# Chunked attention and a gated convolution on one core: another way to decode float64 weights, and a new order of all steps

## The chip, the cores and the metric

The kernel runs on one core of a Trainium2 chip. The core has five engines that work through a queue of their own each: TensorE (PE; its weight loads are PEld), VectorE (DVE), ScalarE (ACT), GpSimd (POOL), and SyncE (SP), which here only issues DMAs. Engines wait for each other through semaphores. The metric is device time in microseconds (us) of one execution; the time before is the median of three runs.

## The reference

q, k and v have shape (4, 8, 768, 64): batch, heads, tokens, head size. Tokens are cut into 24 chunks of 32. Each chunk of queries sees a window of 64 keys: 8 memory keys, 16 to its left, its own 32, and 8 to its right.

```python
scores = scale * np.matmul(q_c, k_full.transpose(0, 1, 3, 2))
scores = scores - np.max(scores, axis=-1, keepdims=True)
a = np.exp(scores)
a = a / (np.sum(a, axis=-1, keepdims=True) + 1e-09)
out[:, :, c_start:c_end] = np.matmul(a, v_full)
...
for k in range(K):
    gate_pre += conv_w[k][None, None, :] * xp[:, k:k + S, :]
gate = 1.0 / (1.0 + np.exp(-gate_pre))
val = x @ w_val
return (gate * val @ w_out).astype(np.float32)
```

The attention output of all heads, x with 512 columns, goes through a causal convolution of five taps per column (the gate) and through two 512 x 512 matrices. These two, `w_val` and `w_out`, and the taps `conv_w` arrive as float64: the kernel reads each number as two 32-bit words and has to make a float32 of them on the chip.

## The kernel before, in words

**Attention by units.** A unit is one pair of heads over one span of tokens. Batch 0 is cut into two spans (256 and 512 tokens), the other batches have one of 768, which makes 20 units: 0 to 3 with 256 tokens, 4 to 7 with 512, 8 to 19 with 768. For a unit u the steps are: load k, q and v (`lk`, `lq`, `lv`), transpose k and q on TensorE (`tk`, `tq`) and copy them out of PSUM (`ek`, `eq`), scores (`sc`), maximum, shift and exponential (`mx`, `ss`, `ex`), transpose the weights of the softmax (`tp`, `ep`), times v (`va`), denominator, inverse, normalise (`nd`, `ni`, `nx`), transpose x (`tx`), split it into a high and a low float32r part (`xh`, `xl`), and five taps of the convolution on the vector engine (`cv`), then tanh (`ga`).

**Matrices by pieces.** Eight pieces of 256, 512 and 384 tokens go through the first matrix (`f1_n_...`), the gate (`h`), another split (`hh`, `hl`), the second matrix (`f2_n_...`), a copy out of PSUM (`oe`) and a store (`st`). Each product is three float32r matmuls: high times high, low times high, high times low.

**Weights.** A matrix is loaded in four row blocks of 128 x 512 float64, 512 KB each: `lw0` to `lw3` for `w_val`, `lw4` to `lw7` for `w_out`, with two raw buffers. Block `wv2`, say, is decoded in eight steps `wv21` to `wv28` (`float64_steps`, L344 to L402), then split into high and low (`wv2h`, `wv2`). Before the change, steps 1, 2, 3, 6 and 7 are vector passes over 128 x 512 (L355, L361, L366, L377, L382), steps 4 and 5 are on ScalarE (L371, L374), and step 8 is a float multiplication on GpSimd (L388).

**What sets the order.** The text `ORDER` lists every step once as `engine:step`; each engine issues its steps in the order in which they stand there, and DMAs are issued by the queue that is named (S for SP, G for POOL, A for ACT). `Plan.run` only sees to it that a step's needs stand ahead of it. An engine is strictly in order: if its next instruction waits, everything behind it waits too. PSUM has one buffer for transposes of q, k and the softmax (`t`), one for scores and value products (`a`), two for `tx` and three for the matrices.

Of the kernel before, what the change touches and what calls it, by code (L numbers as in the profile page):

```python
# [11 lines left out]
U32 = mybir.dt.uint32  # L12
AF = mybir.ActivationFunctionType
# [3 lines left out]
P = 128  # L17
# [3 lines left out]
NEG = -1.0e30  # L21
CAPS = dict(
# [52 lines left out]
V:wv0h V:nd0 G:wv0 V:wv13 T:tp1_0 S:lq3 V:ni0 A:mk2 A:ep1_0 V:nx0 S:lmv A:wv15 T:tk2_0 S:lk3 V:ek2_0
T:va1 T:tx0_0 V:nd1 V:ni1 A:xh0_0 V:wv21 T:tq2_0 A:eq2_0 A:mk3 S:lk4 G:wv18 S:lv2_0 V:nx1 S:lq5
V:wv22 A:wv1h V:mv4 V:cv0_0_4 T:tq3_0 A:eq3_0 G:mv3 V:wv23 T:sc2 V:mx2 A:wv24 V:wv26 T:tx1_0 V:ss2
V:cv0_0_0 A:cv1_0_4 G:lw3 G:wv1 S:lv2_1 T:tk3_0 A:ek3_0 V:cv0_0_1 A:ex2 T:tk4_0 A:wv25 S:lv3_0 T:sc3
V:wv27 V:xl0_0 S:lv3_1 A:ek4_0 T:tp2_0 V:cv1_0_0 A:ep2_0 V:mx3 V:cv1_0_1 V:ss3 V:wv31 A:wv34
V:cv0_0_2 V:cv1_0_2 G:wv28 T:va2 V:nd2 V:wv32 S:lw4 A:ex3 T:tq5_0 V:wv36 S:lq4 A:wv2h A:hs0 V:ni2  # L80
V:cv0_0 V:nx2 A:hs1 V:cv1_0 S:lk5 A:eq5_0 S:lk6 T:tp3_0 A:ep3_0 V:wv33 T:tx2_0 V:wv37 A:ga1 A:xh1_0
A:xh2_0 G:wv2 T:va3 T:tq4_0 S:lv4_1 T:f1_0_10 V:wo01 V:cv2_0_4 A:wv35 G:wv38 A:wo04 A:eq4_0 V:wo02
T:f1_0_00 V:nd3 V:wo03 V:ni3 T:tk5_0 V:xl1_0 A:wo05 A:ga0 S:lq6 G:mv5 A:ek5_0 V:nx3 S:lw5 A:wv3h
V:wo06 V:xl2_0 T:sc4 V:cv2_0_0 V:cv2_0_1 V:wo07 V:mx4 S:lv5_1 V:hs2 T:tx3_0 T:f1_0_11 V:ss4
A:cv3_0_4 S:lv4_0 T:tk6_0 T:sc5 A:ex4 V:cv3_0_0 A:ek6_0 T:tp4_0 T:f1_0_12 A:ep4_0 V:cv3_0_1 G:wv3
V:wo11 T:f1_0_01 V:mx5 V:wo12 V:ss5 A:wo14 A:xh3_0 V:cv2_0_2 T:tq6_0 V:wo13 A:eq6_0 V:cv2_0 A:ex5
# [12 lines left out]
V:wo36 T:tq9_0 T:f2_0_11 S:lq10 A:mk9 T:f1_1_01 A:eq9_0 V:wo37 G:wo2 A:cv6_1_4 A:wo35 V:nd7 V:xl6_0
T:tk9_0 T:f2_0_12 A:ek9_0 A:mk8 T:tk9_1 V:cv6_0_0 V:ni7 V:nx7 T:f2_0_02 G:wo38 V:cv6_1_0 A:xh6_1  # L100
A:ek9_1 V:cv6_0_1 V:cv6_1_1 A:wo3h V:xl6_1 G:wo3 T:tq9_1 A:eq9_1 T:sc8 V:cv6_1_2 V:cv6_0_2 V:cv6_1
V:cv6_0 T:tq10_0 T:f1_1_02 T:tx7_0 V:mx8 V:ss8 S:lv8_0 S:lk11 A:eq10_0 T:tx7_1 T:tq10_1 V:cv7_1_4
T:f2_0_03 A:xh7_0 A:eq10_1 V:xl7_0 G:mv10 V:hp7 T:sc9 A:ex8 A:oe0_0 T:tp8_0 V:xh7_1 A:cv7_0_4
V:cv7_1_0 S:lv8_1 V:xl7_1 S:lk10 A:ep8_0 T:f1_1_03 T:tp8_1 V:mx9 V:ss9 V:cv7_0_0 A:ep8_1 T:f2_0_13
# [79 lines left out]
def tile_chunked_attention_gated_conv(  # L184
# [794 lines left out]
```

## Time and profile before

| | |
|---|---|
| median of 3 runs | 269.98 us (266.08 to 270.07) |
| profiled execution, first to last instruction (span) | 269.1 us |
| PE busy | 238.3 us |
| DVE busy | 218.2 us |
| ACT busy | 127.9 us |
| POOL busy | 80.0 us |
| read from and written to HBM | 28.03 MB and 6.29 MB |

The page gives no other time for the profiled execution than its span, which is 0.9 us under the median of the runs. A busy share is a mean over the whole execution, and here the stretches differ: the table of stretches among the rows below is what to read first, each stretch with the busy time of each engine in it.

### The profile page before, as it was taken

What the parts mean: (1) busy time and instruction counts of PE and PEld (TensorE: products, weight loads), DVE (VectorE), ACT (ScalarE), POOL (GpSimd) and SP (SyncE); (2) the same over time, 40 slices, a digit from 0 to 9 for tenths busy, and PEclk for the clock granted to TensorE, in tenths of its full rate; (3) what the DMA queues carried; (4) which work ended last, traced back from release to release, by engine and by line L of the source; (5) the groups of instructions that cost most, each with busy time, mean ns of one, the idle gap of its engine ahead of it and who ended that gap; (6) DMA issues with size and microseconds to landing.
All of it is one profiled execution on the core that took longest, in us unless ns stands there. A gap on an engine that the chain in (4) does not pass through costs nothing.

```text
span 269.1 us, 9694 instructions
## 1 busy us (share of the span) xinstructions
PE 238.3 (89%) x4158; PEld 200.2 (74%) x4158; DVE 218.2 (81%) x462; ACT 127.9 (48%) x259; POOL 80.0 (30%) x93
## 2 busy tenths in 40 slices
PE   1576586796899996999999999999999999999994
PEld 1343376675678885778998878889998877899883
DVE  3799999899999995997976996999978989893310
ACT  4545574676866745555451515474432443521021
POOL 5473363146460044430105512200322120015100
PEclk9999997979999999999999999999999999999998
DMA  6788999499999899159897991398870061201213
GB/s 151 177 198 207 211 178 183 117 210 180 177 137 147 144 186 178 44 132 137 165 164 132 160 149 55 106 163 187 101 143 2 4 168 44 80 0 39 78 48 111
DMA packets 99601, 34.96 MB, mean 130 GB/s; under 512 B 96082, under 2 KB 96358, under 8 KB 99558
## 3 DMA queue, kind: packets, MB, share of 16 engines
q1 hardware_dynamic: 96710, 29.75, 62.7%
q0 software_dynamic: 1248, 4.20, 4.6%
q8 instruction: 33, 0.54, 0.9%
q10 hardware_dynamic: 1600, 0.39, 0.8%
q14 instruction: 10, 0.08, 0.1%
HBM read 28.03 MB, written 6.29 MB: 128 GB/s over the span
## 4 chain that ended last, share of the span: by engine, by line
PE 76%; DVE 12%; ACT 3%; issue 3%; DMA 3%; SPq 1%; POOL 1%; ACTq 0%; DVEq 0%
PE op L903 25%; PE vp L848 24%; PE sp L639 6%; PE xps L690 6%; PE tpx L750 4%; PE tq L569 4%; PE tk L569 4%; PE tp L569 4%; DVE gate L798 2%; DMA qn<-in_q_dram 2%; DVE e_wo L382 1%; DVE xn L713 1%; DVE e_wo L355 1%; SPq L493 1%; DMA craw<-in_moe_conv_w_dram 1%
## 5 line engine op out<-in xcount | busy, mean ns | idle before, releaser
L798 DVE SCALAR_TENSOR_TENSOR gate<-tpx,cw,gate 128x384 f32<-128x384 f32 (+9 forms) x144 | 79.3, 563 | 1.3 <-ACT gate L802 0.2
L264 POOL TENSOR_TENSOR hl<-h,hh 128x384 fp32r<-128x384 f32 (+2 forms) x25 | 26.0, 1044 | 107.6 <-DVE hh L249 55.2
L848 PE MATMUL vp<-xh,wv_hi 128*128 128x384 f32 (+2 forms) x128 | 49.1, 384 | 0.0
L848 PE MATMUL vp<-xl,wv_hi 128*128 128x384 f32 (+2 forms) x128 | 43.9, 343 | 0.0
L848 PE MATMUL vp<-xh,wv_lo 128*128 128x384 f32 (+2 forms) x128 | 43.9, 343 | 0.0
L903 PE MATMUL op<-wo_hi,hh 128*128 128x512 f32 (+1 forms) x100 | 41.9, 419 | 0.0
L903 PE MATMUL op<-wo_lo,hh 128*128 128x512 f32 (+1 forms) x100 | 38.6, 386 | 0.2 <-POOL wo_lo L264 0.2
L903 PE MATMUL op<-wo_hi,hl 128*128 128x512 f32 (+1 forms) x100 | 38.5, 385 | 0.0
L639 PE MATMUL sp<-kT,qT 64*32 64x64 f32 x1536 | 21.7, 239 | 8.7 <-DVE ss L664 3.9
L639 PEld LDWEIGHTS sp<-kT,qT 64*32 64x32 f32 x1536 | 17.6, 113 | 15.0 <-issue 8.4
L848 PEld LDWEIGHTS vp<-xh,wv_hi 128*128 128x128 f32 x128 | 25.0, 195 | 2.0
L854 DVE SCALAR_TENSOR_TENSOR h<-gate,vp 128x384 f32<-128x384 f32 (+2 forms) x32 | 17.2, 548 | 10.9 <-PE vp L848 9.4
L848 PEld LDWEIGHTS vp<-xh,wv_lo 128*128 128x128 f32 x128 | 25.1, 196 | 0.9
L848 PEld LDWEIGHTS vp<-xl,wv_hi 128*128 128x128 f32 x128 | 24.8, 194 | 0.9 <-DVE xl L264 0.2
L690 PE MATMUL xps<-v,pT 64*32 64x65 f32 x1536 | 21.1, 233 | 4.3 <-ACT pT L246 2.5
L690 PEld LDWEIGHTS xps<-v,pT 64*32 64x32 f32 x1536 | 17.3, 109 | 9.8 <-issue 6.1
L246 ACT COPY pT<-tp 128x384 f32<-128x384 f32 (+2 forms) x27 | 12.9, 479 | 23.5 <-PE tp L569 23.3
L569 PE MATMUL tk<-ident,kn 128*128 128x128 f32 x96 | 18.2, 304 | 6.2 <-ACT memT L246 2.6
L802 ACT ACTIVATE gate<-tpx,cw 128x384 f32<-128x384 f32 (+1 forms) x27 | 14.6, 549 | 15.1 <-PE tpx L750 10.0
L903 PEld LDWEIGHTS op<-wo_hi,hl 128*128 128x128 f32 x100 | 18.8, 188 | 4.0
L252 POOL COPY v<-mv 104x1536 f32<-104x1536 f32 (+2 forms) x12 | 17.4, 1458 | 11.5 <-issue 9.9
L569 PE MATMUL tq<-ident,qn 128*128 128x128 f32 x96 | 18.8, 311 | 2.1 <-DMA qn<-in_q_dram 0.9
(93 smaller groups left out, 423.7 us busy)
## 6 DMA issues: line engine op xcount, KB each, us to landing
qn<-in_q_dram SPq DMA_DIRECT2D x24, 192.0 KB
kn<-in_k_dram SPq DMA_DIRECT2D x24, 192.0 KB
v<-in_v_dram SPq DMA_DIRECT2D x24, 192.0 KB
v<-in_v_dram SPq DMA_DIRECT2D x23, 144.0 KB
out_dram<-o POOLq DMA_DIRECT2D x12, 256.0 KB, 4.0
out_dram<-o SPq DMA_DIRECT2D x11, 256.0 KB
raw_wo<-in_moe_w_out_dram SPq DMA_DIRECT2D x4, 512.0 KB
kn<-in_k_dram SPq DMA_DIRECT2D x12, 96.0 KB
```

Of the source, the lines that this page charges most:

```text
L246: return lambda: nc.scalar.copy(out(), in_())
L252: return lambda: nc.gpsimd.tensor_copy(out(), in_())
L264: return lambda: eng.tensor_tensor(out=out(), in0=a(), in1=b(), op=ALU.subtract)
L569: nc.tensor.transpose(U[name, i][:, (g - g0) * P : (g - g0 + 1) * P], src(g), ident)
L639: nc.tensor.matmul(U["sp"][CH * jc : CH * (jc + 1), j, g * WIN : (g + 1) * WIN], U["qT"][j * D : (j + 1) * D, g * P + CH * jc : g * P + CH ...
L690: nc.tensor.matmul(U["xps"][CH * jc : CH * (jc + 1), j, g * VW : (g + 1) * VW], U["pT"][j * D : (j + 1) * D, g * P + CH * jc : g * P + CH ...
L750: nc.tensor.transpose(U["x", i][:, o : o + P], U["xn"][:, g].rearrange("p j d -> p (j d)"), ident,)
L798: nc.vector.scalar_tensor_tensor(out=o, in0=i_, scalar=w, in1=o, op0=ALU.mult, op1=ALU.add)
L802: nc.scalar.activation(o, i_, AF.Copy, scale=w)
L848: nc.tensor.matmul(vp, w, x, start=ci == 0 and m == 0, stop=ci == NCT - 1 and m == 2)
L854: nc.vector.scalar_tensor_tensor(out=T["h", n, co][:, 0:nt], in0=bt[b, co]["gate"][:, t0 : t0 + nt], scalar=1.0, in1=T["vp", n, co][:, 0:n ...
L903: nc.tensor.matmul(op, x, w[:, ci, c0:c1], start=ci == 0 and m == 0, stop=ci == NCT - 1 and m == 2)
```

## The change

The decoding takes six passes in place of eight. ScalarE reads the high word as a float32, takes its absolute value times 2^-48 (`head`) and turns the low word into an integer of the last bits (`tail`). VectorE keeps the result in bounds (`bounds`), shifts it by three bits (`shifted`) and puts the sign in (`signed`). GpSimd adds the two as 32-bit integers (`rounded`). The small constants that the old passes needed, and their two steps, are gone.

```diff
-        def part1():
-            R["e"] = buf([np_, n], f"e{sfx}", f"e_{name}", U32)
...
-            nc.vector.tensor_scalar(
-                out=R["e"], in0=raw()[:, :, 1], scalar1=20, scalar2=0x7FF,
-                op0=ALU.logical_shift_right, op1=ALU.bitwise_and,
+        def head():
...
+            nc.scalar.activation(
+                R["e"], raw()[:, :, 1].bitcast(F32), AF.Abs, scale=2.0**-48
             )
-        def part2():
+        def bounds():
             nc.vector.tensor_scalar(
-                out=R["m"], in0=raw()[:, :, 1], scalar1=0xFFFFF, scalar2=None, op0=ALU.bitwise_and
+                out=R["e"], in0=R["e"], scalar1=FLOOR, scalar2=CEIL, op0=ALU.max, op1=ALU.min
             )
-        def part3():
-            nc.vector.scalar_tensor_tensor(
-                out=R["mf"], in0=raw()[:, :, 0], scalar=2.0**-32, in1=R["m"], op0=ALU.mult, op1=ALU.add
-        def part4():
-            nc.scalar.activation(R["ef"], R["e"], AF.Relu, bias=bias_e[0:np_], scale=E23)
-        def part5():
-            nc.scalar.activation(R["mf"], R["mf"], AF.Identity, bias=one[0:np_], scale=2.0**-20)
-        def part6():
+        def tail():
+            nc.scalar.activation(R["r"], raw()[:, :, 0], AF.Copy, scale=2.0**-29)
+        def shifted():
             nc.vector.tensor_scalar(
-                out=R["e"], in0=R["ef"], scalar1=255 * E23, scalar2=None, op0=ALU.min
+                out=e, in0=e, scalar1=3, scalar2=None, op0=ALU.logical_shift_left
             )
-        def part7():
+        def signed():
             nc.vector.scalar_tensor_tensor(
-                out=R["e"], in0=raw()[:, :, 1], scalar=0x80000000, in1=R["e"],
+                out=e, in0=raw()[:, :, 1], scalar=0x80000000, in1=e,
                 op0=ALU.bitwise_and, op1=ALU.bitwise_or,
             )
-        def part8(eng):
-            eng.tensor_tensor(out=R["mf"], in0=R["mf"], in1=R["ef"], op=ALU.mult)
+        def rounded():
+            nc.gpsimd.tensor_tensor(
+                out=R["r"], in0=R["e"].bitcast(I32), in1=R["r"], op=ALU.add
+            )
-        step(name + "1", {"V": part1}, after=[load[0], "bias"], takes=bufs, uses=rawbuf)
+        step(name + "1", {"A": head}, after=[load[0]], takes=bufs, uses=rawbuf)
...
 ORDER = """
-G:ident V:bias0 S:mem A:bias S:lcw T:tmem A:lk0 V:cw1 A:cw4 A:emem01 S:lq1 A:emem00 V:emem11
+G:zm G:ident V:zv2 S:mem T:tmem A:lk0 V:zk G:lcw G:zv1 A:emem00 A:emem10 V:zv0 A:cw1 A:cw2 S:lq0
```

The whole table of the order is new. Three places of it follow.

VectorE, block `wo0` of the second matrix. Names: `e_wo0` and `m_wo0` are the two work tiles of the decoding, `raw_wo0` the float64 words, `gate02` a tile of the convolution, `den3` and `xn3` the normalisation of unit 3. Before:

```order
L355 TENSOR_SCALAR e_wo0_550<-raw_wo0_478 128x512
L804 TENSOR_SCALAR gate02_553<-tpx2_0_512,cw_77 128x256
L361 TENSOR_SCALAR m_wo0_551<-raw_wo0_478 128x512
L706 TENSOR_SCALAR den3_565<-xps3_522 128x2x2
L366 SCALAR_TENSOR_TENSOR m_wo0_551<-raw_wo0_478,m_wo0_551 128x512
L709 RECIPROCAL den3_565<-den3_565 128x2x2
L264 TENSOR_TENSOR xl01_573<-tpx1_0_388,xh01_517 128x256
L713 TENSOR_TENSOR xn3_582<-xps3_522,den3_565 128x2x2x64
L377 TENSOR_SCALAR e_wo0_550<-e_wo0_550 128x512
```

And now:

```order
L645 TENSOR_TENSOR ss3_460<-sp3_439,mx3_457 128x2x2x64
L352 TENSOR_SCALAR e_wo0_463<-e_wo0_463 128x512
L361 TENSOR_SCALAR e_wo0_463<-e_wo0_463 128x512
L687 TENSOR_SCALAR den2_503<-xps2_481 128x2x2
L690 RECIPROCAL den2_503<-den2_503 128x2x2
L694 TENSOR_TENSOR xn2_511<-xps2_481,den2_503 128x2x2x64
L367 SCALAR_TENSOR_TENSOR e_wo0_463<-raw_wo0_377,e_wo0_463 128x512
```

Three passes stand where five stood (the fifth of before, L382, comes four rows later), and only the last of them reads the raw words.

ScalarE, blocks `wv2` and `wv3`. `tk`, `tq`, `tp` and `tpx` are PSUM tiles that TensorE fills, `kT` and `qT` what is copied out of them. Before:

```order
L246 COPY qT3_362<-tq3_0_359 128x256
L371 ACTIVATE e_wv2_333<-e_wv2_333,bias_e_83 128x512
L802 ACTIVATE gate01_394<-tpx1_0_388,cw_77 128x256
L246 COPY kT3_71<-tk3_0_402 128x12x2x16
L672 ACTIVATE ss2_391<-ss2_391 128x256
L374 ACTIVATE m_wv2_334<-m_wv2_334,one_84 128x512
L246 COPY kT0_68<-tk4_0_409 128x12x2x16
```

And now:

```order
L347 ACTIVATE e_wv2_284<-raw_wv2_245 128x512
L357 ACTIVATE m_wv2_285<-raw_wv2_245 128x512
L245 COPY v0_72<-mv_78 104x8x64
L783 ACTIVATE gate00_298<-tpx0_0_289,cw_77 128x256
L245 COPY kT2_70<-tk2_0_294 128x12x2x16
L347 ACTIVATE e_wv3_324<-raw_wv3_252 128x512
L245 COPY qT2_344<-tq2_0_335 128x256
```

ScalarE has as many decoding passes as before, but they now read the raw words themselves, so it is this engine's queue that waits for a block to land, and copies out of PSUM stand behind.

SP, the start of the queue. `wv0` and `wv1` are the raw blocks. Before:

```order
L297 DMA mk_nat_76<-in_mem_k_dram 128x2x64
L439 DMA craw_86<-in_moe_conv_w_dram 20x256
L493 DMA qn1_112<-in_q_dram 128x2x64 x2
L493 DMA qn0_132<-in_q_dram 128x2x64 x2
L411 DMA raw_wv0_137<-in_moe_w_val_dram 128x1024
L411 DMA raw_wv1_139<-in_moe_w_val_dram 128x1024
```

And now:

```order
L289 DMA mk_nat_76<-in_mem_k_dram 128x2x64
L474 DMA qn0_122<-in_q_dram 128x2x64 x2
L392 DMA raw_wv1_125<-in_moe_w_val_dram 128x1024
L474 DMA qn1_127<-in_q_dram 128x2x64 x2
L474 DMA v0_72<-in_v_dram 16x64
```

The taps and block `wv0` went to POOL's queue, the keys of unit 1 came from ACT's queue to SP's, and blocks `wv2` and `wv3`, which POOL issued, are now issued by SP as well.

## Rows read from the trace of the kernel before

**Rows 1.** The page: busy tenths in 40 slices, bandwidth of slices

```profile
PE   1576586796899996999999999999999999999994
DVE  3799999899999995997976996999978989893310
GB/s 151 177 198 207 211 178 183 117 210 180 177 137 147 144 186 178 44 132 137 165 164 132 160 149 55 106 163 187 101 143 2 4 168 44 80 0 39 78 48 111
```

**Rows 2.** Stretches: length, then busy of PE, PEld, DVE, ACT, POOL, clock, DMA share, GB/s

```profile
0.00:8.50 8.50, 2.04 (x6) 0.97 (x6) 2.79 (x9) 3.38 (x8) 5.49 (x20) 1.00 0.71 194
8.50:76.60 68.10, 50.52 (x963) 38.29 (x967) 65.15 (x149) 43.41 (x98) 31.71 (x29) 0.95 0.96 175
76.60:101.90 25.30, 25.30 (x643) 20.75 (x643) 24.44 (x53) 15.36 (x30) 5.85 (x5) 1.00 1.05 162
101.90:104.10 2.20, 0.09 (x10) 0.02 (x3) 0.03 (x1) 1.13 (x2) 0.99 (x1) 1.00 1.09 196
104.10:265.50 161.40, 160.35 (x2555) 140.16 (x2554) 125.84 (x253) 64.14 (x121) 35.91 (x40) 1.00 0.52 102
265.50:269.10 3.60, 0.00 (x0) 0.00 (x0) 0.00 (x0) 0.52 (x2) 0.00 (x0) 0.76 0.30 109
```

**Rows 3.** Chain of waits, 71 to 75 us: start, length, what

```profile
71.99 0.51 ACT wo_hi L246
...
72.57 1.71 POOL wo_lo L264
```

**Rows 4.** Timeline of PE: transpose of unit 9's keys, scores of unit 8

```profile
73.45 0.49 PE L569 MATMUL tk<-ident,kn 128*128 128x128 f32 x3
...
76.55 1.17 PE L639 MATMUL sp<-kT,qT 64*32 64x64 f32 x96
```

**Rows 5.** Stretch 8.5 to 76.6, line 355 alone: length, DVE busy, clock, DMA

```profile
8.50:76.60 68.10, 5.04 (x8) 0.95 0.96 175
```

**Rows 6.** The same stretch, line 361 alone

```profile
8.50:76.60 68.10, 3.31 (x8) 0.95 0.96 175
```

**Rows 7.** The same stretch, line 366 alone

```profile
8.50:76.60 68.10, 6.75 (x8) 0.95 0.96 175
```

**Rows 8.** Groups by shape, DVE, 8.5 to 76.6: count, busy, mean ns, idle before

```profile
L249 DVE COPY v<-mv 104x1024 f32<-104x1024 f32 x1 | 3.0, 2966 | 0.0
...
L377 DVE TENSOR_SCALAR e_wo<-e_wo 128x512 uint32<-128x512 f32 x4 | 1.8, 445 | 0.0
...
L249 DVE CAST wv_hi<-m_wv 128x512 fp32r<-128x512 f32 x1 | 0.4, 414 | 0.0
```

**Rows 9.** Groups by shape, whole execution: DVE, POOL and ACT

```profile
L264 DVE TENSOR_TENSOR hl<-h,hh 128x384 fp32r<-128x384 f32 x7 | 4.5, 641 | 1.2 <-ACT hh L246 1.2
...
L388 POOL TENSOR_TENSOR m_wo<-m_wo,e_wo 128x512 f32<-128x512 f32 x4 | 5.2, 1296 | 3.6 <-ACT tpx L246 3.6
...
L371 ACT ACTIVATE e_wo<-e_wo,bias_e 128x512 f32<-128x512 uint32 x4 | 2.9, 732 | 0.0
```

**Rows 10.** Timeline of DVE and POOL, 33 to 68 us: single passes

```profile
33.42 0.68 DVE L382 SCALAR_TENSOR_TENSOR e_wv<-raw_wv,e_wv 128x512 uint32<-128x512 uint32 x1
...
43.20 0.42 DVE L355 TENSOR_SCALAR e_wo<-raw_wo 128x512 uint32<-128x512 uint32 x1
...
60.99 1.27 POOL L264 TENSOR_TENSOR wo_lo<-m_wo,wo_hi 128x512 fp32r<-128x512 f32 x1 [2.72 <-ACT wo_hi L246]
...
61.28 1.52 DVE L382 SCALAR_TENSOR_TENSOR e_wo<-raw_wo,e_wo 128x512 uint32<-128x512 uint32 x1
...
66.88 1.29 POOL L388 TENSOR_TENSOR m_wo<-m_wo,e_wo 128x512 f32<-128x512 f32 x1
66.95 1.50 DVE L355 TENSOR_SCALAR e_wo<-raw_wo 128x512 uint32<-128x512 uint32 x1
```

**Rows 11.** DMA up to 76.6 us: packets, bytes, mean rate, packets under a size

```profile
DMA packets 38338, 13.54 MB, mean 177 GB/s; under 512 B 37283, under 2 KB 37303, under 8 KB 38327
```

**Rows 12.** Waits of PE, 8.5 to 76.6 us: total, times, longest

```profile
PE tq L569 <- DMA qn<-in_q_dram: 0.9, 1, 0.9
```

More of the change, by code (lines that the diff above doesn't have):

```diff
@@ L12 @@
 U32 = mybir.dt.uint32
+I32 = mybir.dt.int32
 AF = mybir.ActivationFunctionType
@@ L21 @@
 NEG = -1.0e30
+FLOOR = 2.0**-63
+CEIL = (1.875 - 2.0**-23) * 2.0**-32
 CAPS = dict(
@@ L75 @@
[L75 to L86, printed above, removed]
@@ L99 @@
[L99 to L104, printed above, removed]
@@ new lines @@
+V:cv5_1_1 V:cv5_1_2 A:ga4 A:ep7_0 T:tx6_0 A:hp6 A:cv6_0_4 T:tk8_0 A:xh6_0 G:wo38 A:ek8_0 V:cv5_1
+T:f2_0_02 T:va7 V:nd7 V:ni7 A:wo3h T:tq9_0 A:eq9_0 T:tx6_1 A:cv6_1_4 V:cv6_0_0 S:lq10 V:xl6_0
+A:xh6_1 V:cv6_0_1 G:hl0_3 S:lk11 T:f1_1_01 T:tk9_0 A:ek9_0 V:nx7 V:cv6_1_0 V:xl6_1 G:wo3 T:f2_0_13
+A:oe0_1 V:cv6_0_2 T:tk9_1 A:ek9_1 T:sc8 T:tq9_1 T:f2_0_03 A:eq9_1 V:cv6_0 A:oe0_0 T:tx7_1 A:xh7_1
+A:cv7_1_4 V:cv6_1_1 V:cv6_1_2 T:tq10_0 A:eq10_0 V:mx8 V:cv6_1 V:ss8 V:xl7_1 V:cv7_1_0 T:f1_1_02
+V:cv7_1_1 V:cv7_1_2 T:tx7_0 A:xh7_0 A:ex8 T:f1_1_10 G:mv9 A:hp7 V:xl7_0 T:tq10_1 S:lv8_0 S:lv8_1
@@ L180 @@
+T:f2_6_03 V:oe6_0 G:st6_0 T:f1_7_30 T:f2_6_23 A:oe6_2 T:f1_7_31 T:f2_6_10 T:f2_7_10 T:f2_6_11
+T:f1_7_32 T:f2_6_12 T:f1_7_33 V:h7_3 G:hl7_2 A:hh7_3 V:hl7_3 T:f2_7_11 T:f2_6_13 V:oe6_1 S:st6_1
+T:f2_7_12 G:st6_2 T:f2_7_20_ T:f2_7_13 T:f2_7_00 A:oe7_1 T:f2_7_21_ T:f2_7_01 T:f2_7_22_ T:f2_7_02
+T:f2_7_23_ V:oe7_2_ T:f2_7_20 T:f2_7_03 A:oe7_0 S:st7_1 T:f2_7_21 T:f2_7_22 T:f2_7_23 S:st7_0
+A:oe7_2 S:st7_2 G:st7_2_
 """
@@ L232, in tile_chunked_attention_gated_conv @@
     wo_lo = const.tile([P, NCT, DM], F32R, name="wo_lo")
-    bias_e = const.tile([P, 1], F32, name="bias_e")
-    one = const.tile([P, 1], F32, name="one")
-    ones = const.tile([P, 1], F32, name="ones")
     plan = Plan(dict(CAPS))
@@ L264, in minus @@
         return lambda: eng.tensor_tensor(out=out(), in0=a(), in1=b(), op=ALU.subtract)
-    def biases():
-        nc.vector.memset(bias_e, -896 * E23)
-        nc.vector.memset(ones, 1.0)
-    E23 = 2.0**23
     step("ident", {"G": lambda: make_identity(nc, ident)})
-    step("bias0", {"V": biases})
-    step("bias", {"A": lambda: nc.scalar.copy(one, ones)}, after=["bias0"])
     def zero_k(eng):
@@ L385, in part7 @@
             )
-        def part8(eng):
-            eng.tensor_tensor(out=R["mf"], in0=R["mf"], in1=R["ef"], op=ALU.mult)
+        def rounded():
+            nc.gpsimd.tensor_tensor(
+                out=R["r"], in0=R["e"].bitcast(I32), in1=R["r"], op=ALU.add
+            )
         rawbuf = load[1]
-        step(name + "1", {"V": part1}, after=[load[0], "bias"], takes=bufs, uses=rawbuf)
-        step(name + "2", {"V": part2}, after=[name + "1"], uses=rawbuf)
-        step(name + "3", {"V": part3}, after=[name + "2"], uses=rawbuf)
@@ L394, in float64_steps @@
-        step(name + "4", {"A": part4}, after=[name + "1"])
-        step(name + "5", {"A": part5}, after=[name + "3"])
-        step(name + "6", {"V": part6}, after=[name + "4"])
-        step(name + "7", {"V": part7}, after=[name + "6"], uses=rawbuf)
-        step(
-            name + "8",
-            {"G": lambda: part8(nc.gpsimd), "V": lambda: part8(nc.vector)},
-            after=[name + "5", name + "7"], uses=bufs,
-        )
+        step(name + "1", {"A": head}, after=[load[0]], takes=bufs, uses=rawbuf)
@@ L403, in float64_steps @@
+        step(name + "2", {"A": tail}, after=[name + "1"], uses=rawbuf)
+        step(name + "3", {"V": bounds}, after=[name + "1"])
+        step(name + "4", {"V": shifted}, after=[name + "3"])
+        step(name + "5", {"V": signed}, after=[name + "4"], uses=rawbuf)
+        step(name + "8", {"G": rounded}, after=[name + "2", name + "5"], uses=bufs)
         return bufs
```

199 lines of the change are left out of this document (103 added, 96 removed).

## The prediction

> **What bounds the kernel now.** I read the table of stretches first [rows 2], since the page's line of slices shows PE with gaps in the first 12 of 40 slices and full after that, and DVE full from the second slice on [rows 1]. The stretches split the span of 269.1 us as follows. Up to 8.5 us everything starts up. From 8.5 to 76.6 DVE is busy 65.15 of 68.10 us and PE only 50.52: DVE is the bound, and PE loses 17.6 us. From 76.6 to 101.9 both are full (24.44 and 25.30 of 25.30). Then PE stands still for 2.2 us with no engine to blame. From 104.1 to 265.5 PE is busy 160.35 of 161.40: nothing but less PE work could shorten that, and the change removes no matmul. The last 3.6 us are the final copy and store. The chain of waits says the same for the end of the second stretch: PE is let go there by the decoding of a block of the second matrix, a copy on ACT and a subtraction on POOL [rows 3].
>
> So the place to look at is the step `sc8`, the scores of the first 768-token unit, which starts at 76.55 [rows 4]. The two written orders have nearly the same matmuls ahead of it (the change has one step of the second matrix more and one transpose of queries less). If `sc8` starts x us sooner, and PE stays as full behind it as it is now, the end comes x us sooner.
>
> **What the change takes from DVE ahead of `sc8`.** Eight blocks are decoded in this stretch.
> - Removed: the shift-and-mask of the exponent, 5.04 us [rows 5], the mask of the mantissa, 3.31 [rows 6], and the pass that adds the low word, 6.75 [rows 7]: 15.10 us.
> - Kept in another form: the old minimum becomes `bounds`, the pass that sets the sign becomes `signed`, with the same shapes; I count no difference.
> - Added: `shifted`, eight passes in place over 128 x 512. The trace has no such shift. The nearest row is the in-place pass L377 with 0.445 us; the bounds are 0.414 (a plain pass of that size) [rows 8] and 1.50 (a pass of L355 while POOL was at work) [rows 10]. I take 0.445: 3.56 us.
> - Moved away: a copy of memory values on DVE, 2.97 us [rows 8], goes to POOL or ACT.
> - Moved here: two subtractions `wv_lo` from POOL. A vector subtraction of two SBUF tiles of 128x384 takes 0.641 [rows 9], so 0.85 for 512 columns: 1.70 us. Of small copies four come and two go, at about 0.414 [rows 8]: 0.83 us.
> - The sum is -15.10 + 3.56 - 2.97 + 1.70 + 0.83 = -12.0 us.
>
> **What goes to other engines.** ACT keeps two passes per block; one takes 0.732 [rows 9], and reading every second word could cost more. ACT has 24.7 us idle in the stretch [rows 2], so 16 passes with up to 0.4 more each hide there. If that cover went, 6.4 us would count. POOL's float product becomes an integer sum; the product takes 1.296 [rows 9]. It could be faster, and my upper bound is 1.71, the slowest subtraction of that shape [rows 3]; only the last two blocks stand right ahead of a PE wait, so 0 to 0.8 us reach the end, and I take 0. The two clearings of v buffers that come to DVE, and the two constants that go, lie before 8.5, where DVE is idle for 5.7 us [rows 2]: nothing. On SP's queue, the keys of unit 1 and two raw blocks come in, the taps and one block go out; I take 0 for the issues themselves, with the bound of the loads below as the check. In the tail, the last half tile is stored by POOL, while two groups of matmuls still run: 0.
>
> **What is late next.** If DVE alone decided, `sc8` would start at 76.55 - 12.0 = 64.6. The loads come next. By the kernel's shapes 11.85 MB must have landed before `sc8` in the new order: 4.19 for eight blocks, 2.36 keys, 2.36 queries, 2.86 values, and 0.08 of small things. In the trace 1.65 MB came by 8.5 us, and then 175 GB/s [rows 2]; up to 76.6, 13.54 MB were moved [rows 11]. At this rate 11.85 MB are there at 8.5 + 10.20/0.175 = 66.8. From the transposes of unit 9's keys to `sc8` took 3.1 us [rows 4], so the loads allow `sc8` at 69.9, a gain of 6.7. DVE allows a gain of 12.0. The rate of 175 is itself that of an order in which queues waited for buffers, and slices with over 200 exist [rows 1]; I put the forecast nearer to the loads, at a gain of 8: `sc8` at 68.5.
>
> **The forecast** is then 269.1 - 8 = 261.1 for the span, and with the 0.9 us by which the median of the runs lies above it, **262.0 us**.
>
> **A rule that speaks against the change.** The vector pass that reads two SBUF tiles, L382, takes 0.68 while POOL is idle and 1.52 while POOL runs, and a pass with one input, L355, takes 0.42 or 1.50 in the same way [rows 10]. The in-place pass L377 has a mean of 0.445 [rows 8], so it is hardly touched. The Trainium skill, GPSIMD Engine Reference, section Specifications, says that GpSimd shares its SBUF interfaces with VectorE and contends with vector instructions that have two SBUF inputs or run in a two-port mode. By that rule the new shift would be slowed as L355 is; the trace agrees for L382 and for some passes of L355, and not for L377. What it would make of the time is the third rival.
>
> **The rivals.**
> 1. *DVE's gain arrives whole, and the 2.2 us stall goes too.* For: PE has little else to wait for, and the stall names no engine. Against: the loads. 269.98 - 12.0 - 2.2 = 255.8 us.
> 2. *The loads decide.* In the stretch after 76.6, where the queues never rest, they bring only 162 GB/s at a share of 1.05 [rows 2]. At 162, `sc8` comes at 8.5 + 10.20/0.162 + 3.1 = 74.6, a gain of 2.0: 268.0 us. For: 37283 of 38338 packets are under 512 B [rows 11] and the DMA share of the stretch is already 0.96 [rows 2]. Against: PE's longest wait on a load in the stretch is 0.9 us [rows 12]. The Trainium skill, DMA: Bandwidth & Descriptors, section Specifications, gives 512 B as the least size for full rate; no run here shows larger packets for the same loads.
> 3. *Vector passes and POOL contend.* POOL is busy 31.71 of 68.10 us, 47% [rows 2]. If the 16 passes of `bounds` and `shifted` took 1.50 in that share of cases, they would cost 16 x 0.47 x 1.06 = 7.9 us more; the gain would be 4.1: 265.9 us.
> 4. *ScalarE waits for the raw blocks, slower than before.* The first decoding pass now stands in ACT's queue and waits for a block of 512 KB, with copies out of PSUM behind it; there is one buffer for transposes, so PE stops too. At 175 GB/s a block takes 3.0 us. Six blocks are loaded while PE works. If each is late by its whole transfer, ACT and with it PE lose 18 us: 269.98 - 12.0 + 18 = 276 us. It comes out slower than before beyond the limit below from 2.9 us per block on. Against: the passes of DVE that read these words before follow the work ahead of them without a gap [rows 10], so the blocks were there.
> 5. *The change does not do what it says*: counting PSUM waits in the order saves nothing or sets up new ones, and what DVE gains is lost in PE waits elsewhere: about 270 us.
>
> **The numbers.** The forecast gets 0.42, the rivals 0.20, 0.14, 0.10, 0.09 and 0.05. A difference of under 2% (5.4 us) can hardly be told from none. Faster by that, under 264.6: nine tenths of the forecast's cases, the first rival, and 0.04 from rivals 2 and 3, together 0.62. Slower, over 275.4: rival 4, 0.09. The rest is 0.29. The forecast's own range is 258 to 265.5, from DVE's bound (258.0) to the loads' bound (263.3) and the unknown passes behind it. The whole range, 257 to 269, takes in rivals 2 and 3 and half of rival 1; it leaves out rival 4, rival 5 and the other half.
>
> **What would show it.** In the new profile no vector pass over the raw words but `signed` is left, `shifted` is near 0.45, and DVE's sum falls by over 15 us; `sc8` starts at 66 to 70; PE is full from about 70 us to the last matmul; the last 3.6 us stay. The forecast is wrong if `sc8` starts after 72, or if PE has gaps of over 3 us in total after it, or if ACT shows waits on raw blocks; a load as releaser of PE before `sc8` would speak for rival 2, and passes of 1.5 us in `shifted` for rival 3.

## The result, and the profile after

The changed kernel takes **256.35 us** (median of 4 runs, 254.66 to 258.14). The kernel before took 268.31 us beside it (4 runs, 266.08 to 270.07). The ratio is **0.9576, with an interval of 0.9492 to 0.9661**, so it is 3.4% to 5.1% faster. The forecast was 262.0 us with a range of 257 to 269: the direction was right, the gain was larger, and the time lies 0.65 us under the range. A second set of 4 runs gave 257.68 us, ratio 0.9588 (0.9517 to 0.966). Ratios and their intervals, here and below, leave out executions more than 1.5% above the fastest of their kernel, among them one of 324.83 us of `e3_bounds_thrice` at a granted clock of 0.69, while medians have them all.

The profiled execution has a span of 256.3 us and its own time was 258.14, so 1.84 us lie around the span. The page in 40 slices, lines of three engines or rates, answering to [rows 1]:

```profile
PE   2477596789999999999999999999999999999994
DVE  5878879699997998989589967997798978833120
GB/s 171 184 235 160 177 240 148 172 223 181 213 125 166 181 232 97 186 144 178 199 144 73 107 173 197 169 99 220 40 113 3 43 43 87 83 2 0 82 80 87
```

PE is full from the tenth slice on (6.4 us each), where it was full from the twelfth on but for one (6.7 us each), and DVE shows fewer nines in front. The stretches, with the columns of [rows 2], cut at the scores of unit 8 and at the end of the last matmul:

```profile
0.00:8.50 8.50, 2.46 (x8) 1.26 (x8) 5.38 (x21) 3.48 (x9) 4.27 (x11) 1.00 0.72 193
8.50:68.10 59.60, 46.55 (x956) 35.84 (x954) 50.92 (x132) 39.52 (x93) 27.12 (x25) 0.94 0.96 193
68.10:252.80 184.70, 184.30 (x3198) 161.00 (x3197) 141.42 (x279) 92.11 (x179) 42.16 (x46) 1.00 0.61 116
252.80:256.30 3.50, 0.00 (x0) 0.00 (x0) 0.00 (x0) 0.38 (x1) 0.00 (x0) 1.00 0.31 115
```

Two things are to be seen. The second stretch ends 8.45 us sooner than in [rows 2] and [rows 4] (68.10 against 76.55), with DVE busy 50.92 of 59.60 us where it was 65.15 of 68.10. And in the third PE is idle for 0.40 us of 184.70. The same cut in the kernel before, from the scores of unit 8 to the end of the span:

```profile
76.55:269.10 192.55, 185.79 (x3198) 160.98 (x3197) 150.35 (x306) 81.14 (x153) 42.75 (x45) 1.00 0.60 111
```

From there to the end it took 192.55 us before and takes 188.20 now: 4.35 of the 12.8 us that the span lost were won behind the place that the prediction looked at.

The groups of the new decoding by shape in 8.5 to 68.1 us (count, busy us, mean ns, idle before) answer to [rows 8, 9]:

```profile
L373 POOL TENSOR_TENSOR m_wo<-e_wo,m_wo 128x512 int32<-128x512 int32 x4 | 5.4, 1356 | 12.3 <-DVE e_wo L367 12.3
...
L367 DVE SCALAR_TENSOR_TENSOR e_wv<-raw_wv,e_wv 128x512 uint32<-128x512 uint32 x4 | 3.9, 966 | 0.1
...
L367 DVE SCALAR_TENSOR_TENSOR e_wo<-raw_wo,e_wo 128x512 uint32<-128x512 uint32 x4 | 2.8, 731 | 0.0
...
L347 ACT ACTIVATE e_wo<-raw_wo 128x512 f32<-128x512 f32 x4 | 2.7, 671 | 2.2 <-DMA raw_wo<-in_moe_w_out_dram 2.2
...
L361 DVE TENSOR_SCALAR e_wv<-e_wv 128x512 uint32<-128x512 uint32 x4 | 1.8, 458 | 0.0
L361 DVE TENSOR_SCALAR e_wo<-e_wo 128x512 uint32<-128x512 uint32 x4 | 1.7, 421 | 0.0
L352 DVE TENSOR_SCALAR e_wv<-e_wv 128x512 f32<-128x512 f32 x4 | 1.7, 420 | 0.6 <-ACT e_wv L347 0.6
...
L263 DVE TENSOR_TENSOR wv_lo<-m_wv,wv_hi 128x512 fp32r<-128x512 f32 x2 | 1.7, 828 | 0.0
```

The chain of waits up to the scores of unit 8 (start, length, what) has loads as its longest pieces, where the last pieces of the one before were decoding [rows 3]:

```profile
14.95 3.73 DMA mv<-in_mem_v_dram
...
23.70 5.51 DMA raw_wo<-in_moe_w_out_dram
...
36.41 7.26 DMA v<-in_v_dram
...
44.41 5.65 DMA v<-in_v_dram
...
50.20 0.85 PE xps L671 x48
...
68.17 1.10 PE sp L620 x72
```

Added up by engine, loads make 31.4 and DVE 2.9 of the 68.1 us of this chain (15.6 and 13.0 of 65.98 in the second execution below); in two executions of the kernel before loads make 6.8 and 12.5, and DVE 32.3 and 33.3.

Up to 68.1 us the queues moved 13.12 MB at a mean of 193 GB/s, against 177 up to 76.6 [rows 11].

### The profile page after: what moved, and what is told of

The parts are those of the page before. It is cut to its first block, busy times and chain, and to the rows that moved or that the text cites. A ratio compares the mean times of both kernels' runs of the same rounds, so it can differ in the third digit from the quotient of the medians.

```text
span 256.3 us, 9684 instructions
## 1 busy us (share of the span) xinstructions
PE 233.3 (91%) x4158; PEld 198.1 (77%) x4158; DVE 197.7 (77%) x430; ACT 135.5 (53%) x280; POOL 73.6 (29%) x81
## 4 chain that ended last, share of the span: by engine, by line
PE 79%; DMA 12%; ACT 2%; SPq 2%; issue 2%; DVE 1%; POOL 1%; ACTq 0%; POOLq 0%
PE op L884 26%; PE vp L829 24%; PE xps L671 6%; PE sp L620 6%; DMA v<-in_v_dram 5%; PE tpx L731 5%; PE tp L550 4%; PE tk L550 4%; PE tq L550 4%; DMA raw_wo<-in_moe_w_out_dram 2%; DMA kn<-in_k_dram 2%; DMA raw_wv<-in_moe_w_val_dram 2%; DMA mv<-in_mem_v_dram 1%; SPq L474 1%; ACT kT L245 1%
## 5 line engine op out<-in xcount | busy, mean ns | idle before, releaser
L779 DVE SCALAR_TENSOR_TENSOR gate<-tpx,cw,gate 128x384 f32<-128x384 f32 (+8 forms) x144 | 79.8, 564 | 3.0 <-ACT gate L783 0.9
L829 PE MATMUL vp<-xh,wv_hi 128*128 128x384 f32 (+2 forms) x128 | 48.5, 379 | 0.0
L835 DVE SCALAR_TENSOR_TENSOR h<-gate,vp 128x384 f32<-128x384 f32 (+2 forms) x32 | 17.4, 549 | 14.3 <-PE vp L829 14.2
L251 POOL COPY v<-mv 104x1536 f32<-104x1536 f32 (+1 forms) x13 | 17.8, 1371 | 29.6 <-PE xps L671 23.5
L245 ACT COPY kT<-tk 128x384 f32<-128x384 f32 x30 | 14.4, 479 | 17.7 <-PE tk L550 17.6
L620 PE MATMUL sp<-kT,qT 64*32 64x64 f32 x1536 | 20.5, 230 | 3.1 <-DVE ss L645 1.9
L620 PEld LDWEIGHTS sp<-kT,qT 64*32 64x32 f32 x1536 | 16.7, 108 | 8.4 <-issue 3.2
L245 ACT COPY qT<-tq 128x384 f32<-128x384 f32 (+2 forms) x30 | 14.6, 485 | 15.4 <-PE tq L550 15.3
L783 ACT ACTIVATE gate<-tpx,cw 128x384 f32<-128x384 f32 (+1 forms) x32 | 17.5, 548 | 9.0 <-PE tpx L731 8.8
```

The lines of the kernel that those rows point to most:

```text
L245: return lambda: nc.scalar.copy(out(), in_())
L251: return lambda: nc.gpsimd.tensor_copy(out(), in_())
L620: nc.tensor.matmul(U["sp"][CH * jc : CH * (jc + 1), j, g * WIN : (g + 1) * WIN], U["qT"][j * D : (j + 1) * D, g * P + CH * jc : g * P + CH ...
L779: nc.vector.scalar_tensor_tensor(out=o, in0=i_, scalar=w, in1=o, op0=ALU.mult, op1=ALU.add)
L783: nc.scalar.activation(o, i_, AF.Copy, scale=w)
L829: nc.tensor.matmul(vp, w, x, start=ci == 0 and m == 0, stop=ci == NCT - 1 and m == 2)
```

## The experiments

"Scores" below is the start of the scores of unit 8, read from the timeline of PE as in [rows 4]. Rows of stretches have the columns of [rows 2]. Ratios are to the kernel before, run on the same chip.

**How much two executions of one kernel differ.** `b2_before_again` is the kernel before once more, `a2_after_again` the changed one.

> The kernel before, once more, for a second profile. Of the 3.06 us that PE stood still between the scores of unit 8 and its last matmul, 2.2 us were one stop with no engine to blame. If that stop belongs to the order (theory A), it is there again within 0.5 us, near 102 us. If it is chance of one execution (theory B), it is gone or elsewhere, and the span is some 2 us shorter.

> The changed kernel once more: a second profile and three more rounds beside the same kernel before. Theory A (stops belong to the order): PE stands still for less than 0.5 us after the scores of unit 8. Theory B: a stop of 1 to 3 us can show. Time 254 to 258.

The one run of before took 267.68 us, that of after 257.68 (median of 4). The two stretches up to the scores and behind them, before:

```profile
0.00:73.73 73.73, 50.04 (x962) 36.45 (x962) 65.62 (x157) 46.73 (x106) 37.20 (x48) 1.00 0.92 182
73.73:265.90 192.17, 185.78 (x3198) 160.91 (x3197) 150.43 (x306) 81.17 (x153) 42.80 (x45) 1.00 0.60 112
```

and after:

```profile
0.00:65.98 65.98, 48.60 (x961) 36.89 (x961) 56.39 (x152) 42.92 (x101) 31.44 (x36) 0.95 0.94 198
65.98:254.50 188.52, 184.28 (x3198) 161.01 (x3197) 141.47 (x279) 92.68 (x180) 42.23 (x46) 1.00 0.62 116
```

The scores move by 2 to 3 us from one execution to the next in either kernel, so a difference of less than that between two profiles proves nothing. The part behind the scores moves less: 192.2 to 192.6 before, 188.2 to 188.5 after. Its gain, 3.65 to 4.35 us, stands in both pairs. TensorE's granted clock differs too: up to the scores it was 0.96, as a mean, in the first execution of before and 1.00 in the second, and the same 962 matmuls kept PE busy for 52.50 and 50.04 us. That this alone made the first one late is not shown: in the changed kernel the clock was 0.95 both times, and its scores still differ by 2.1 us.

**The new decoding in the old order.** `e1_decode_only` has the new passes, and the old table with each old step's name replaced by the new pass that does its work: steps 1 to `head` on ACT, 3 to `tail`, 4 to `bounds`, 6 to `shifted`, 7 to `signed`; step 2, 5 and the constants' steps drop out.

```diff
-... V:eq0_0 G:zv2 V:wv01 V:mk0 T:tq1_0 S:lv1_1 V:mk1 A:wv04 A:eq1_0 V:wv02 V:wv11 G:cw8 T:sc0 ...
+... V:eq0_0 G:zv2 A:wv01 V:mk0 T:tq1_0 S:lv1_1 V:mk1 V:wv03 A:eq1_0 A:wv11 G:cw8 T:sc0 ...
```

> The order of before, with the new decoding in the places of the old passes (two vector passes per block fewer, the low word's pass now on ScalarE where the third vector pass stood). Theory 1, less vector work decides: 11.5 us less DVE work ahead of the scores of unit 8, which then start at 66 to 70 us; time 258 to 261. Theory 2, the new order decides: the scores start at 74 us or later, time 266 or more. Theory 3, both are needed, since ScalarE now waits for raw blocks at places chosen for something else: 262 to 265.

It took 266.92 us, ratio 0.9931 (0.9873 to 0.999). The two stretches:

```profile
8.50:74.26 65.76, 48.72 (x954) 37.45 (x953) 52.29 (x132) 42.28 (x97) 28.68 (x26) 0.97 0.88 181
74.26:264.40 190.14, 185.75 (x3198) 161.22 (x3197) 150.51 (x306) 81.08 (x153) 42.83 (x45) 1.00 0.56 113
```

DVE is relieved by 10.7 to 12.9 us against the two executions of before (62.99 and 65.15 in the same stretch), and the scores come at 74.26, between the two executions of before (73.73 and 76.55). DVE waits instead; its longest waits up to the scores (what waited, for whom, us in total, times, longest):

```profile
DVE sp L637 <- PE sp L620: 3.4, 3, 1.7
DVE den L687 <- PE xps L671: 2.9, 2, 2.3
DVE gate L785 <- ACT xh L245: 1.9, 1, 1.9
DVE kT L248 <- PE tk L550: 1.1, 1, 1.1
```

The theory that DVE's amount of work alone decides fell here: DVE was full before, and yet taking a sixth to a fifth of its work away moved nothing at the scores. A second bound stood right behind it. The chain up to the scores is made of 22.4 us of PE, 17.8 of DVE, 13.8 of loads and 11.5 of ACT: no engine holds it alone. Some of these hand-overs came with the new passes: PE waits 2.0 and 1.4 us for decoding passes on ACT here. How much of the second bound is the old order's own, and how much comes of new passes in places chosen for others, no run separates.

**The new order with the old decoding.** `e2_order_only` has the old passes and the new table, with the names replaced the other way round.

```diff
-... S:lv0_1 T:tq1_0 A:eq1_0 V:wv13 V:wv14 V:wv15 A:wv01 T:sc0 V:mx0 V:ss0 ...
+... A:wv14 V:wv13 A:wv15 V:wv16 V:wv17 V:wv01 T:sc0 V:mx0 V:ss0 ...
```

> The new order, with the old decoding put in the places of the new passes. Theory 1: DVE has 11.5 us more to do ahead of the scores of unit 8 than in the changed kernel, they start at 76 to 80 us, time 265 to 269. Theory 2: they start at 70 us or before, time 258 or less. Whatever the start, PE's stops after it: if they come from the order they stay under 0.5 us here.

It took 268.36 us, ratio 0.9968 (0.9929 to 1.0008).

```profile
8.50:79.00 70.50, 50.50 (x961) 38.60 (x959) 60.69 (x154) 42.33 (x96) 27.96 (x25) 0.98 0.77 162
79.00:267.80 188.80, 183.93 (x3198) 160.51 (x3197) 141.53 (x279) 92.84 (x180) 41.82 (x45) 1.00 0.71 116
```

The front is worse (79.00), the part behind as good as in the changed kernel (188.80). DVE is busy 60.69 of 70.50 us, not full: it waits 5.6 us for value products of PE, and PE waits 4.6 us for one copy on DVE and 2.6 for one on ACT. The places of the new table were chosen for other passes. So this run shows that the order is worth its gain in front only with the new passes; what another order for the old passes could do it does not show.

Alone, then, the decoding gives 0.7% and the order 0.3%, the latter not to be told from nothing. Together they give 4.2%.

**More work for DVE, in either order.** `e3_bounds_thrice` does the bounds pass of each of the eight weight blocks three times (the values stay the same): 16 passes more, about 6.6 us of DVE. `e6_old_order_bounds_thrice` does the same in `e1_decode_only`.

```diff
-            nc.vector.tensor_scalar(
-                out=R["e"], in0=R["e"], scalar1=FLOOR, scalar2=CEIL, op0=ALU.max, op1=ALU.min
-            )
+            for _ in range(3 if np_ == P else 1):
+                nc.vector.tensor_scalar(
+                    out=R["e"], in0=R["e"], scalar1=FLOOR, scalar2=CEIL, op0=ALU.max, op1=ALU.min
+                )
```

> The changed kernel with the bounds pass of each weight block done three times in place of once (the result is the same): 16 vector passes of 0.41 us more, 6.6 us, all ahead of the scores of unit 8. Theory 1, in the new order DVE sets the pace of the start: the scores go from 66 to 68 us to 72 to 74, time 261 to 264. Theory 2, in the new order something else does (loads, copies out of PSUM) and DVE has that much to spare: the scores stay under 69, time 256 to 258.

> The old order with the new decoding, and the same 16 vector passes more (6.6 us), which brings DVE's work ahead of the scores of unit 8 to 62 us, still under the 66 to 68 of the kernel before. Theory 1, DVE's work as such sets the pace: scores at 78 to 81 us. Theory 2, the old order has slack on DVE that it cannot use: scores at 74 to 76 us, time 264 to 268, as without the added passes.

In the new order: 258.88 us, ratio 0.9647 (0.9569 to 0.9725). That is 1.2 to 2.5 us over the two medians of the changed kernel, and the intervals overlap.

```profile
8.50:67.83 59.33, 44.98 (x955) 34.53 (x954) 57.16 (x148) 39.43 (x93) 27.31 (x25) 0.97 0.95 194
```

In the old order: 271.52 us, ratio 1.0129 (1.0054 to 1.0203).

```profile
8.50:78.50 70.00, 47.63 (x953) 35.96 (x953) 59.20 (x148) 42.10 (x98) 28.43 (x26) 0.98 0.81 170
```

The same 16 passes (DVE's busy time grew by 6.2 and 6.9 us) cost the scores nothing in the new order (67.83 against 68.10 and 65.98) and 4.2 us in the old one (78.50 against 74.26). In the old order DVE was by then busy for only 59.20 us, less than the 65.15 of the kernel before, and the scores came later. So in the old order with the new passes the sum of DVE's work does not set the scores: the passes lie in a chain of hand-overs, where each counts although DVE rests elsewhere.

**Fewer bytes ahead, in three kernels.** `e4_fewer_v` is the changed kernel, `e5_old_order_fewer_v` is `e1_decode_only` and `e8_before_fewer_v` the kernel before, each without the loads of the last 24 keys of v's windows (1.2 MB less ahead of the scores; that part of the output is not computed).

```diff
-                loads.append((t[e0 : r0 + WIN, 0:c1, 0:D], window(LEFT, LEFT + RIGHT, 0, c1)))
+                pass
```

> The changed kernel without the loads of the values right of each chunk's own 32 (24 of 56 rows of v, so 1.2 MB of 11.85 ahead of the scores of unit 8, and 43% of the bytes of v later; these keys then meet zeros or old values). At 193 GB/s, 1.2 MB are 6 us. Theory 1, loads are the bound of the new order's start: scores at 60 to 64 us, time 250 to 253. Theory 2, DVE or PSUM is: scores at 65 to 68 us, time 254 to 258.

> The old order with the new decoding, and the same loads left out. Theory 1, with less vector work the old order is held by its loads: scores of unit 8 at 68 to 70 us in place of 74, time 258 to 262. Theory 2, it is held by the sequence of transposes and copies through the one PSUM buffer: scores stay at 73 to 75 us, time 263 to 266. The stops of PE inside the scores after that: if a full DMA queue makes them, none over 0.3 us is left.

> The kernel before, old decoding and old order, without the loads of the last 24 keys of v's windows (that part of the output is not computed). Theory 1 (DVE's amount of work bounds the kernel before, as the prediction read it from 65 of 68 us busy): the scores of unit 8 stay at 73.7 to 76.6 and the time within 1.5 us of before, ratio 0.995 to 1.0. Theory 2 (the loads hold the chain of hand-overs back there too, and DVE's busy share is no bound): the scores come 3 us sooner and the time falls by 3 to 4.5 us, as with the new decoding in the old order, ratio 0.983 to 0.989.

The changed kernel: 251.27 us, ratio 0.9382 (0.9311 to 0.9453).

```profile
8.50:61.27 52.77, 44.37 (x956) 34.17 (x954) 50.67 (x132) 39.61 (x93) 27.16 (x25) 0.97 0.82 196
61.27:249.20 187.93, 184.10 (x3198) 160.92 (x3197) 141.28 (x279) 92.63 (x180) 42.20 (x46) 1.00 0.39 97
```

The scores come at 61.27, 4.7 to 6.8 us sooner than in the two executions of the changed kernel, and what follows is as long as there. 1.2 MB at its 193 GB/s are 6.2 us. So the loads are the bound of the changed kernel's front. DVE is now busy 50.67 of 52.77 us: it stands next.

The old order with the new decoding: 262.65 us, ratio 0.9803 (0.9738 to 0.9869).

```profile
8.50:71.21 62.71, 48.36 (x953) 37.23 (x953) 51.80 (x132) 42.22 (x97) 28.84 (x26) 0.95 0.69 165
```

The scores gain 3.0 us, as much as two executions can differ by, but the time gains too: the interval lies below that of `e1_decode_only` (0.9873 to 0.999). They stop at 71.21, with DVE busy 51.80 of 62.71: with loads and DVE both relieved, the old order still comes 9.9 us later than the new one.

The kernel before: 265.47 us, ratio 0.9934 (0.9897 to 0.9971).

```profile
8.50:73.15 64.65, 47.94 (x956) 35.29 (x956) 62.53 (x149) 43.23 (x98) 32.10 (x29) 1.00 0.74 161
73.15:263.30 190.15, 185.58 (x3198) 160.82 (x3197) 150.38 (x306) 81.12 (x153) 42.74 (x45) 1.00 0.42 96
```

Here neither theory held whole. The scores at 73.15 are 0.6 us ahead of the earlier of two executions of before, with DVE busy 62.53 of 64.65, and DVE makes 54.2 us of the chain up to them: that is what theory 1 says, DVE is the bound there. The time fell all the same, by 0.3% to 1.0%, which is 0.8 to 2.8 us, and of the 2.6 us between this span and that of `b2_before_again` 2.0 were won behind the scores.

**Both at once.** `e7_fewer_v_bounds_thrice` has the edits of `e4_fewer_v` and `e3_bounds_thrice` together.

> The new kernel without the loads of the last 24 keys of v's windows (that part of the output is not computed; 251.27 us, scores of unit 8 at 61.27) and with the bounds pass of each of the eight weight blocks done three times (16 more DVE passes, about 6.6 us). Theory 1 (once the loads are out of the way, DVE's amount of work is the next bound of the new order, since DVE is idle for only 0.6 us there): the scores of unit 8 go from 61.3 to 66 to 68, the time to 255.5 to 258. Theory 2 (the chain of hand-overs between ACT, PE and DVE decides, and DVE has room in it): the scores stay under 63.5, the time under 253.5.

It took 257.32 us, ratio 0.9621 (0.9566 to 0.9675).

```profile
8.50:68.56 60.06, 44.93 (x956) 34.35 (x954) 57.99 (x148) 39.36 (x93) 27.05 (x25) 0.97 0.72 172
68.56:252.40 183.84, 183.84 (x3198) 160.91 (x3197) 141.16 (x279) 92.12 (x179) 42.14 (x46) 1.00 0.39 97
```

Theory 1 held, a little over its size: the 16 passes, free in `e3_bounds_thrice`, now cost 7.3 us at the scores (61.27 to 68.56), as much as DVE's busy time grew (50.67 to 57.99), and 6.05 us of time. With the loads out of the way DVE is the bound, at 57.99 of 60.06 us.

Start of the scores of unit 8 in us, all profiled executions together:

| | all loads | 1.2 MB less |
|---|---|---|
| old order, old decoding | 76.55, 73.73 | 73.15 |
| old order, new decoding | 74.26 | 71.21 |
| old order, new decoding, 16 passes more | 78.50 | |
| new order, old decoding | 79.00 | |
| **new order, new decoding** | **68.10, 65.98** | 61.27 |
| new order, new decoding, 16 passes more | 67.83 | 68.56 |

## Why the prediction was right in front and wrong behind

**DVE's work: right in its main terms.** The sum was -12.0 us, for the stretch from 8.5 us on; there DVE's busy time fell by 14.2 (65.15 to 50.92). Before 8.5 us it grew by 2.6 (2.79 to 5.38), where the prediction counted nothing, so that over the whole way to the scores it fell by 11.6 (67.88 to 56.29); that this lies near -12.0 is luck. Before and after:

```profile
0.00:76.55 76.55, 52.50 (x962) 39.21 (x962) 67.88 (x157) 46.78 (x106) 37.20 (x48) 0.96 0.93 177
...
0.00:68.10 68.10, 49.01 (x962) 37.11 (x962) 56.29 (x152) 43.01 (x101) 31.39 (x36) 0.95 0.93 193
```

Of its terms: `shifted` took 3.51 us in eight passes (taken: 3.56), the two `wv_lo` 1.7 (1.70). The removed passes are all gone. `signed` was to stay at the cost of the old pass L382 and fell from 9.09 to 6.70 us, which the sum did not have: four of the eight old passes took 1.5 to 1.6 us beside work of POOL, where in the changed kernel one took 1.80 and another 0.86, and the other six 0.6 to 0.7.

**The loads come next: right, and shown.** The forecast put the scores at 68.5, between a bound of DVE at 64.6 and one of the loads at 69.9. They came at 68.10 and 65.98. `e4_fewer_v` and `e7_fewer_v_bounds_thrice` show both bounds: without the loads' limit the scores stand at 61.27, where DVE is full. Both bounds were forecast 2 to 4 us too late, so that 68.5, a choice between them, came so near is in part luck. The loads ran at 193 to 198 GB/s, not at the 175 of a front in which queues waited for buffers, although 13.12 MB came where the new order needed 11.85.

**DVE as the bound of the kernel before: right, but half of the story.** `e8_before_fewer_v` says that DVE held the scores there. The working then went from "DVE is full" to "what DVE loses, the scores gain, up to the loads", and that holds for the new order alone. With the new decoding in the old order the scores would not have moved: `e1_decode_only`, `e5_old_order_fewer_v` and `e6_old_order_bounds_thrice` show hand-overs right behind DVE, the old order's own or brought by the new passes in its places, that the profile of before could not show, since DVE's 65.15 of 68.10 covered them. The rival "the change does not do what it says" treated the order as something that saves nothing. It is what turns DVE's freed time into earlier scores. Part of how can be read: the first product with `w_val` starts at 23.83 and with `w_out` at 50.96 in the changed kernel, against 35.09 and 62.82 before and 34.86 and 62.68 in `e1_decode_only`. So PE has matrix work 11 to 12 us earlier, to do while attention steps are handed to and fro. That this early work is the cause is not shown: in `e2_order_only` the first product with `w_val` is early too, at 28.29, and the scores come late. Which of the moved steps brings the gain was not tried alone.

**"PE stays as full behind it as it is now": this step failed.** The part behind the scores went from 192.55 to 188.20 us. Of the 4.35, 2.76 are time in which PE stood still ahead of its last matmul (3.16 from 76.55 to 265.5, now 0.40), 1.49 are shorter busy time of PE, and 0.10 are the tail; in the second pair of executions the 3.65 are 2.05, 1.50 and 0.10. In spans the forecast was 261.1 and 256.3 came; of the 4.8 us between them 0.4 lie at the scores (68.5 against 68.10), and the rest is this step. The stop of 2.2 us was counted as staying; only the first rival let it go. In the timeline of PE (idle time before the row, and its releaser, in brackets) the stops of the kernel before are:

```profile
104.08 0.66 PE L639 MATMUL sp<-kT,qT 64*32 64x64 f32 x42 [2.11 <-issue]
...
121.26 0.42 PE L639 MATMUL sp<-kT,qT 64*32 64x64 f32 x21 [0.47 <-issue]
...
158.12 0.78 PE L639 MATMUL sp<-kT,qT 64*32 64x64 f32 x55 [0.43 <-issue]
```

and in its second execution:

```profile
100.40 0.66 PE L639 MATMUL sp<-kT,qT 64*32 64x64 f32 x42 [1.31 <-issue]
...
117.83 0.42 PE L639 MATMUL sp<-kT,qT 64*32 64x64 f32 x21 [0.75 <-issue]
...
154.64 0.78 PE L639 MATMUL sp<-kT,qT 64*32 64x64 f32 x55 [0.40 <-issue]
```

In the changed kernel one is left in the first execution, and one at another matmul in the second:

```profile
95.83 0.80 PE L620 MATMUL sp<-kT,qT 64*32 64x64 f32 x57 [0.22 <-issue]
...
98.80 0.69 PE L671 MATMUL xps<-v,pT 64*32 64x65 f32 x44 [0.68 <-issue]
```

They wait for nothing that the trace names. In the kernel before they stand at the same matmuls in both executions and differ in length, so neither theory of `b2_before_again` held whole; in the changed kernel they do not, and the 0.68 us miss both theories of `a2_after_again`. The old order does not bring all three by itself: `e1_decode_only`, with the same order of matmuls there, has one of 0.32 us in place of three, and `e6_old_order_bounds_thrice` two, of 0.92 and 0.48. Fewer loads do not end them (0.96 us in `e5_old_order_fewer_v`), and the new order is not free of them (1.15 us in `e3_bounds_thrice`, 0.63 in `e2_order_only`). So their part of the gain, 2.05 to 2.76 us, is measured, but that the change brought it is not shown. A stop that no engine causes should have been put down as a term that can be 0 or 2 to 3 us, with both ends in the range.

The 1.49 us of shorter busy time go with the order: behind the scores PE is busy 185.5 to 186.0 us in the six executions of the old order and 183.8 to 184.3 in the six of the new one. About 0.4 of it is work that changed sides (three matmuls of the second matrix now stand ahead of the scores, three transposes behind them). The rest was not taken apart further.

**What lies around the span.** The prediction took 0.9 us between span and median. In each execution with both on record it is 1.8 (258.14 and 256.3; 267.68 and 265.9). If it was 1.8 there too, the profiled execution of before was not one at the median but, at some 270.9 (269.1 + 1.8), one of the longer ones, and its scores at 76.55 were late. That flatters the change by up to 2.6 us in a comparison of single profiles; the ratios are free of it. Of the 5.65 us by which 262.0 was too long, 1.67 are the median of before, 268.31 with a fourth run in place of 269.98, and the other 4.0 are gain that was not forecast.

**The rivals.** The first came within 0.6 us of the time (255.8), with half of its mechanism: the stop went, but the scores gained 8.45 us, not 12.0, so its number is near by luck. The second was wrong in its rate of 162 and right in that the loads are the next bound: PE's waits for keys and values are 2.0 and 1.3 us in the stretch, where its longest for a load was 0.9 [rows 12]. The third did not come, but its mechanism is there: `bounds` and `shifted` have means of 409 to 458 ns because they hardly ever meet POOL. It is busy 27.12 us of the stretch, and yet only three of the 16 passes overlap with it, one of them begun behind POOL's instruction (0.57 us); the share of 47% in which the rival let them meet was wrong. A pass that begins while an instruction of POOL runs ends 0.27 to 0.29 us after that instruction, as in `a2_after_again` and `e1_decode_only`:

```profile
10.16 1.27 POOL L373 TENSOR_TENSOR m_wv<-e_wv,m_wv 128x512 int32<-128x512 int32 x1 [1.16 <-DVE sp L637]
...
11.00 0.71 DVE L352 TENSOR_SCALAR e_wv<-e_wv 128x512 f32<-128x512 f32 x1
...
34.70 1.04 POOL L251 COPY v<-mv 104x1024 f32<-104x1024 f32 x1
...
34.93 1.09 DVE L352 TENSOR_SCALAR e_wo<-e_wo 128x512 f32<-128x512 f32 x1 [0.16 <-ACT e_wo L347]
```

Alone such a pass takes 0.42, and a pass that began before POOL's instruction took that too. The mean of 0.445 that the prediction read as "hardly touched" is that of four passes, two of which met POOL, 0.25 and 0.13 us before its instruction ended. The Trainium skill, GPSIMD Engine Reference, section Specifications, has GpSimd and VectorE contend for their SBUF interfaces where a vector instruction has two SBUF inputs or a two-port mode. The trace agrees for the two-input `signed`, 0.69 alone and 1.80 beside a subtraction on POOL; which mode the one-input passes run in, it does not say. The fourth was small: ACT waits for raw blocks 2.2 + 2.2 us in the stretch, not 18, and PE waits for one of these passes 2.2 us; such waits were named as a sign that the forecast is wrong, and they came without the loss. The fifth named new PE waits, and the stretch has none that loses what DVE gained.

## What to carry to other kernels

An engine at 96% busy can be the bound and relieving it can still gain next to nothing: before the gain is counted, ask which hand-overs of the written order lie under its busy time, and test the freed engine in the old order and the new order with the old work, since here 0.7% and 0.3% became 4.2% only together. A bound is found by pushing it: repeating a cheap pass and leaving out a load told which of DVE, loads and hand-overs stood first and which next. A price for two engines that get in each other's way has to be multiplied by how often their instructions meet, and busy shares do not tell that: 45% for POOL here, and one pass in 16 that waited. Give a stop with no releaser both ends, staying and going, and compare two executions of the old kernel before reading a difference of 2 us from single profiles.

## What the runs showed of the hardware that was not expected

- PE's stops without a releaser stand at the same three matmuls in both executions of the kernel before, and their length differs (2.11 and 1.31 us, 0.47 and 0.75); in the changed kernel the places differ too. In the kernel before, a packet of 16 KB on the queue that the page lists as q8, instruction, moved 1.0 to 3.2 us ahead of each of the six stops shown above (between 100.8 and 101.0, say, for the stop from 101.97 to 104.08). Such packets, 33 in an execution, come without a stop too, so a late fetch of instructions is a guess that no run here shows.
- The integer sum of 128 x 512 on GpSimd takes 1273 to 1356 ns (means of four), about as long as the float product of that shape, 1273 to 1296.
- ScalarE reads every second 32-bit word of a block at little extra cost: 661 to 684 ns for a pass over 128 x 512. The old passes on packed words took 724 to 732, but read a second small tile; the exponential, the tanh and the casts, on packed words without one, take 614 to 641.
- A one-input vector pass over 128 x 512 takes 0.42 us alone. One that begins while a sum, subtraction, copy or clearing of GpSimd runs ends 0.27 to 0.29 us after it, in each of 27 single passes found in nine of the executions, and so takes up to 1.50 [rows 10]. One that began before GpSimd's instruction, or with it, kept its 0.42.
